# mLSTM cell and squared-ReLU FFN on one core: h computed with features in the rows, and FFN2 in two halves around FFN1

## Chip, core and metric

One core of a Trainium2 chip; the runs were spread over several chips, and each ratio below is against the kernel before on the same chip. The metric is the device time of the whole kernel in microseconds (us); lower is better. PE is TensorE (PEld its weight loads), DVE VectorE, ACT ScalarE, POOL GpSimd, SP SyncE, whose queue (SPq) issues the DMAs.

## The reference, cut

```python
# mLSTM cell, batch 4, heads 8, seq 768, head_dim 40; per step t:
C = f_stab * C + i_stab * outer(v, k);  n = f_stab * n + i_stab * k
y[:, :, t] = sigmoid(o) * (C q) / max(|n q|, 1)
# then, with x of 3072 tokens x 320:
h = maximum(x @ w_in, 0)        # 320 -> 2048
out = (h * h) @ w_out           # 2048 -> 320
```

## The kernel before: the parts that matter

Attention runs in 24 chunks `s` of 128 tokens (6 to a batch entry). FFN1 and FFN2 work on groups `g` of two chunks. All is float32. In attention, tokens stand in the rows of the result:

```python
def attend(s):                      # cut
    for j in range(PR):             # hi: state x q, 4 matmuls, 82 columns move
        nc.tensor.matmul(hi[:, 2*j:2*j+2, :]..., lhsT=d["qT"][:, j, :], rhs=C[:, j]...)
    for j in range(PR):             # dC: what the chunk adds to the state
        nc.tensor.matmul(dC[:, j]..., lhsT=d["kq"][:, 0, 2*j:2*j+2, :]..., rhs=d["vw"][:, 2*j:2*j+2, :]...)
    for h in range(H):              # hp: weights of 128 columns, 41 columns move
        nc.tensor.matmul(hp[:, h, :], lhsT=d["P"][h % 2][:, h // 2, :], rhs=d["va"][:, h, :])
    ...                             # DVE scales hi, masks dC; POOL adds to the state
```

FFN2 of groups 1 to 11 uses seven products in place of eight, from sums of blocks (`S1`, `S2`, `S4`, one more in place) that DVE makes. The products run in four steps, in two PSUM banks:

```python
elif step == 2:
    product(X5, S1, T[0]);                      add(u22, u22, X5)     # add: DVE reads PSUM
    product(Y6, g4[:, :, 1, cols[1]], T[2]);    add(m1, m1, Y6)
else:
    product(X5, S4, B22);                       add(u12, u12, X5)
```

The main loop deals out parts: four of FFN2(g), then four of FFN1(g+3), and so on. Each chunk of attention spans four parts: scores and P ahead of the first, attend and normalise ahead of the second, exponentials after the third. The sums are made in four short pieces inside FFN1. The order of an engine's instructions matters below: in these traces DVE and the DMA queue take theirs in the order of the program. A few names: `tp` holds the scores (k times q), P is the scores weighted by the decays, which DVE makes, and a *seam* is the stretch in which one group of FFN2 ends and the next begins.

## Time and profile before

| | before |
|---|---|
| time, median of 3 runs | 549.42 us (548.85 to 550.05) |
| span of the profiled run, mean granted clock | 546.6 us, 0.994 |
| PE busy | 537.6 us (98%) |
| DVE busy | 329.9 us (60%) |
| waits of PE for others after 98 us | one, of 0.9 us |

### The profile page before, as it was taken

What the parts mean: (1) busy time and instruction counts of PE and PEld (TensorE: products, weight loads), DVE (VectorE), ACT (ScalarE), POOL (GpSimd) and SP (SyncE); (2) the same over time, 40 slices, a digit from 0 to 9 for tenths busy, and PEclk for the clock granted to TensorE, in tenths of its full rate; (3) what the DMA queues carried; (4) which work ended last, traced back from release to release, by engine and by line L of the source; (5) the groups of instructions that cost most, each with busy time, mean ns of one, the idle gap of its engine ahead of it and who ended that gap; (6) DMA issues with size and microseconds to landing.
All of it is one profiled execution on the core that took longest, in us unless ns stands there. A gap on an engine that the chain in (4) does not pass through costs nothing.

```text
span 546.6 us, 9788 instructions
## 1 busy us (share of the span) xinstructions
PE 537.6 (98%) x3688; PEld 480.9 (88%) x3689; DVE 329.9 (60%) x637; ACT 176.6 (32%) x448; POOL 100.5 (18%) x117
## 2 busy tenths in 40 slices
PE   9989899999999999999999999999999999999997
PEld 5868788887889989989989989989989988979997
DVE  8588988788575575555565565555466456353440
ACT  3767587272242032341131432231423204011000
POOL 2354633233221120111121120101211210000000
PEclk9998999999999999999999999999999999999999
DMA  9998898856653654673565556466554220100000
GB/s 194 223 218 170 167 184 214 165 120 121 123 105 71 117 123 81 118 148 63 109 116 106 108 112 110 81 131 118 100 107 88 45 50 13 42 12 2 26 26 24
DMA packets 226480, 58.07 MB, mean 106 GB/s; under 512 B 185376, under 2 KB 223264, under 8 KB 226432
## 3 DMA queue, kind: packets, MB, share of 16 engines
q1 hardware_dynamic: 226336, 57.24, 52.8%
q8 instruction: 29, 0.48, 0.4%
q10 hardware_dynamic: 96, 0.20, 0.1%
q14 instruction: 19, 0.16, 0.1%
HBM read 49.84 MB, written 13.14 MB: 115 GB/s over the span
## 4 chain that ended last, share of the span: by engine, by line
PE 93%; DVE 4%; ACT 1%; issue 1%; POOL 0%; DVEq 0%; POOLq 0%
PE h_ps L619 31%; PE h_ps L525 29%; PE h_ps L536 8%; PE hp L446 8%; PE tp L409 4%; PE dC L439 3%; PE h_ps L565 3%; PE hi L432 3%; PE idle L682 1%; PE A_ps L348 1%; ACT W_sb L372 1%; DVE mag L203 1%; PE A_ps L344 1%; PE tp L396 1%; DVE g L558 1%
## 5 line engine op out<-in xcount | busy, mean ns | idle before, releaser
L525 PE MATMUL h_ps<-xT,w_in 128*128 128x256 f32 x768 | 175.5, 384 | 1.5 <-DVE xT L501 0.9
L525 PEld LDWEIGHTS h_ps<-xT,w_in 128*128 128x128 f32 x768 | 143.4, 190 | 24.7 <-issue 3.0
L551 ACT ACTIVATE r_sb<-h_ps 128x512 f32<-128x512 f32 x96 | 49.9, 601 | 196.7 <-PE h_ps L536 193.6
L558 DVE TENSOR_TENSOR g<-r_sb 128x512 f32<-128x512 f32 x96 | 62.4, 708 | 56.5 <-ACT r_sb L551 56.5
L619 PE MATMUL h_ps<-w_out,g 128*128 128x160 f32 x528 | 76.9, 302 | 0.0
L619 PEld LDWEIGHTS h_ps<-w_out,g 128*128 128x128 f32 x528 | 72.5, 190 | 1.3 <-ACT r_sb L551 0.3
L372 ACT ACTIVATE W_sb<-A_bc,b_T 128x128 f32<-128x128 f32 x176 | 53.8, 394 | 6.0 <-POOL A_bc L357 5.9
L619 PE MATMUL h_ps<-T,S 128*128 128x160 f32 x352 | 51.4, 299 | 0.0
L536 PE MATMUL h_ps<-xT,w_in 64*128 64x256 f32 x384 | 49.0, 391 | 0.0
L619 PEld LDWEIGHTS h_ps<-T,S 128*128 128x128 f32 x352 | 49.0, 190 | 0.0
L446 PE MATMUL hp<-va,P_sb 128*128 128x41 f32 x368 | 45.7, 286 | 0.0
L536 PEld LDWEIGHTS h_ps<-xT,w_in 64*128 64x128 f32 x384 | 34.8, 186 | 12.3 <-issue 9.0
L383 POOL TENSOR_TENSOR vw<-va,W_sb 128x328 f32<-128x328 f32 x20 | 16.3, 815 | 156.0 <-ACT W_sb L372 130.6
L446 PEld LDWEIGHTS hp<-va,P_sb 128*128 128x128 f32 x368 | 44.6, 198 | 0.0
L633 DVE TENSOR_TENSOR y_sb<-y_sb,h_ps 128x160 f32<-128x160 f32 x33 | 10.6, 320 | 48.9 <-PE h_ps L619 48.9
L465 POOL TENSOR_TENSOR C_sb<-C_sb,Cd 128x328 f32<-128x328 f32 x16 | 14.1, 878 | 124.1 <-DVE C_sb L457 123.8
L633 DVE TENSOR_TENSOR y_sb<-h_ps,y_sb 128x160 f32<-128x160 f32 x22 | 7.1, 324 | 45.1 <-PE h_ps L619 26.4
L421 DVE TENSOR_TENSOR P_sb<-tp,W_sb 128x512 f32<-128x512 f32 x46 | 29.5, 682 | 7.3 <-PE tp L409 6.8
L409 PEld LDWEIGHTS tp<-qT,kT 40*128 40x128 f32 x384 | 24.2, 187 | 3.3 <-issue 2.3
L409 PE MATMUL tp<-qT,kT 40*128 40x128 f32 x384 | 26.9, 279 | 0.0
L642 ACT COPY y_sb<-h_ps 128x160 f32<-128x160 f32 x11 | 3.2, 292 | 70.6 <-PE h_ps L619 70.6
L619 PE MATMUL h_ps<-T,g 128*128 128x160 f32 x176 | 25.7, 299 | 0.0
(100 smaller groups left out, 629.0 us busy)
## 6 DMA issues: line engine op xcount, KB each, us to landing
A_bc<-a_rows SPq DMA_DIRECT2D x22, 512.0 KB, 4.5
raw<-in_moe_w_out_dram SPq DMA_DIRECT2D x16, 320.0 KB, 3.3
raw<-in_moe_w_in_dram SPq DMA_DIRECT2D x8, 512.0 KB, 5.1
kq<-in_k_dram SPq DMA_DIRECT2D x24, 160.0 KB, 3.5
va<-in_v_dram SPq DMA_DIRECT2D x24, 160.0 KB, 4.0
og<-in_o_gate_dram SPq DMA_DIRECT2D x24, 160.0 KB, 3.8
out_dram<-y_sb SPq DMA_DIRECT2D x24, 160.0 KB, 2.5
x_rows<-x_sb SPq DMA_DIRECT2D x18, 192.0 KB, 2.1
```

The lines of the kernel that those rows point to most:

```text
L372: nc.scalar.activation(d["W"][:, i * n + h, :], A[i][:, h, :], AF.Exp, bias=b_T[:, b, c, i * n + h : i * n + h + 1],)
L409: nc.tensor.matmul(sc[i][:, j, :], lhsT=d["kT"][rows, j, :], rhs=d["qT"][rows, j, :], start=True, stop=True,)
L421: nc.vector.tensor_tensor(t, d["sc"][i], d["W"][:].rearrange("p (j two) t -> p j two t", two=2)[:, :, i, :], op=ALU.mult,)
L432: nc.tensor.matmul(hi[:, 2 * j : 2 * j + 2, :].rearrange("p h d -> p (h d)"), lhsT=d["qT"][:, j, :], rhs=C[:, j].rearrange("p h d -> p (h ...
L439: nc.tensor.matmul(dC[:, j].rearrange("p h d -> p (h d)"), lhsT=d["kq"][:, 0, 2 * j : 2 * j + 2, :].rearrange("p h d -> p (h d)"), rhs=d[" ...
L446: nc.tensor.matmul(hp[:, h, :], lhsT=d["P"][h % 2][:, h // 2, :], rhs=d["va"][:, h, :], start=True, stop=True,)
L525: nc.tensor.matmul(hs[i][:, n, :], lhsT=w_in[:, a, fb * P : (fb + 1) * P], rhs=xT[:, :, a, :], start=(n == 0 and a == 0), stop=False,)
L536: nc.tensor.matmul(hs[i][:, n, :], lhsT=w_in2[rows, 2 * pp + n, :], rhs=xT[rows, :, 2, :], start=False, stop=(n == 1),)
L551: nc.scalar.activation(rs[-1][:], h[:], AF.Relu)
L558: nc.vector.tensor_tensor(g4[:, :, i, :], r[:], r[:], op=ALU.mult)
L619: nc.tensor.matmul(to, lhsT=lhsT[:, p], rhs=rhs[:, p, :], start=(start and p == 0), stop=(p == NPAIR - 1), skip_group_check=True,)
L633: add = lambda to, a, b: nc.vector.tensor_tensor(to, a, b, op=ALU.add)
```

## The change

The intent: hp costs 109 ns a pass because 128 columns of weights are loaded to move 41. If v and the state become the weights (64 columns) and P and q move (128 columns), two heads fit beside each other in the array. The result then has features in the rows, so it is turned: DVE transposes 32x32 blocks, a store and four loads through DRAM move the blocks. That takes time, so x comes later, and FFN1 is put between the halves of FFN2. The diff, cut to its core:

```diff
+def attend_turned(s):
+    for j in range(PR):
+        for i in range(2):          # 64x64 tiles (0,0) and (64,64)
+            nc.tensor.matmul(numT[halves[i], j, :], lhsT=C[live[i], j*D1 : j*D1+DP], rhs=d["eA"][live[i], j, :], ...)
+    for j in range(PR):
+        for i in range(2):          # 128x64 tiles side by side
+            nc.tensor.matmul(numT[halves[i], j, :], lhsT=va_w[s % NKQ][:, h*D1 : h*D1+DP], rhs=d["P"][i][:, j, :], ...)
+    ...                             # dC likewise, 40 columns of weights, 41 move
+    nc.vector.transpose(tn..., numT...)
+def scale_q(s):                     # ahead of attend: eA (exponentials, by ACT) times q
+    nc.vector.tensor_tensor(d["eA"], d["eA"], d["qT"], op=ALU.mult)
+def move_num(s):                    # store tn to DRAM, four loads back
+def normalise_turned(s):            # two parts after attend
 ...
 elif step == 2:
-    product(X5, S1, T[0]);  add(u22, u22, X5)
-    product(Y6, g4[:, :, 1, cols[1]], T[2]);  add(m1, m1, Y6)
+    product(Y, g4[:, :, 1, cols[1]], T[2], start=True);  add(m1, u22, Y)
+    product(X, S1, T[0], start=True);  add(u22, u22, X)
 else:
-    product(X5, S4, B22);  add(u12, u12, X5)
+    product(X, S4, B22);  add(u12, u12, X)
 ...
-for g in range(NG):
-    parts += [(2, g, i) for i in range(4)] + FFN1(g + 3)
+for g in range(1, NG):
+    parts += [(2, g, 0), (2, g, 1)] + FFN1(g + 2) + [(2, g, 2), (2, g, 3)]
 ...                                 # and, at step 3 of each group:
+if new_sums:
+    for one in (1, 2, 3):
+        sums(g + 1, slice(0, NPAIR), (one,))
+if at == 3:
+    do(normalise_turned, s); do(store_rows, s)
```

More of the change, by code (lines that the diff above doesn't have):

```diff
@@ L92 @@
     kq_d = nc.dram_tensor("kq_rows", (NT, 2, 2, PR, P, D), F32, kind="Internal").ap()
+    n_d = nc.dram_tensor("num_rows", (NT, P, 4 * P), F32, kind="Internal").ap()
     x_d = nc.dram_tensor("x_rows", (NT, 3, P, P), F32, kind="Internal").ap()
@@ L97 @@
     kq_b = [consts.tile([P, 2, H, DP], F32, name=f"kq{i}") for i in range(NKQ)]
-    va_b = [consts.tile([P, H, D1], F32, name=f"va{i}") for i in range(NKQ)]
-    NKT = 3
-    kT_b = [consts.tile([P, PR, P], F32, name=f"kT{i}") for i in range(NKT)]
+    va_w = [consts.tile([P, H * D1 + 24], F32, name=f"va{i}") for i in range(NKQ)]
+    va_b = [t[:, : H * D1].rearrange("p (h d) -> p h d", d=D1) for t in va_w]
+    NKT = 2
+    kqT_b = [consts.tile([P, 2, PR, P], F32, name=f"kqT{i}") for i in range(NKT)]
     ident = consts.tile([P, P], F32)
-    bdm = consts.tile([P, PR, 2, D1], F32)
+    bdm = conv.tile([P, PR, 2, D1], F32, bufs=1)
     keep = gates.tile([BH, NB, P], F32)
@@ L115, in make_consts @@
             nc.vector.memset(t[:, :, D:], 1.0)
+        for t in va_w:
+            nc.gpsimd.memset(t[:, H * D1 :], 0.0)
         nc.vector.memset(keep[:], 1.0)
@@ L279, in pair_up @@
                 nc.sync.dma_start(
-                    kq_d[s, n, i].rearrange("j (m r) d -> m j (r d)", r=8),
-                    src[b, i::2, c * P : (c + 1) * P, :].rearrange("j (m r) d -> m j (r d)", r=8),
-                )
-    def squares_in(s, n, dst):
-        for i in range(2):
-            for e in range(0, D, SQ):
-                w = min(SQ, D - e)
-                nc.sync.dma_start(
-                    dst[DP * i + e : DP * i + e + SQ].rearrange("p (b a) -> p b a", a=SQ)[:, :, :w],
-                    kq_d[s, n, i, :, :, e : e + w].rearrange("j (m r) a -> r (j m) a", r=SQ),
-                )
-    def q_squares(s):
-        return kq_b[s % NKQ][:, 1].rearrange("p h d -> p (h d)")
+                    kq_d[s, i, n].rearrange("j (m r) d -> m j (r d)", r=8),
+                    src[b, PR * i : PR * (i + 1), c * P : (c + 1) * P, :].rearrange("j (m r) d -> m j (r d)", r=8),
+                )
     def load(s):
@@ L301, in load, with kqT @@
             nc.sync.dma_start(dst, src[b, :, c * P : (c + 1) * P, :].rearrange("h p d -> p h d"))
+    def kqT(s):
+        t = kqT_b[s % NKT]
+        st[s]["kT"], st[s]["qT"] = t[:, 0], t[:, 1]
+        return t
     def load_squares(s):
-        if s < KQ_SQ + NKQ:
-            nc.gpsimd.memset(q_squares(s), 0.0)
-        t = st[s]["kT"] = kT_b[s % NKT]
-        squares_in(s, 0, t[:].rearrange("p j t -> p (j t)"))
-        squares_in(s, 1, q_squares(s))
+        t = kqT(s)[:].rearrange("p n j (m a) -> p (n j m) a", a=SQ)
+        for i in range(2):
+            for e in range(0, D, SQ):
+                w = min(SQ, D - e)
+                nc.sync.dma_start(
+                    t[DP * i + e : DP * i + e + SQ, :, :w],
+                    kq_d[s, i, :, :, :, e : e + w].rearrange("n j (m r) a -> r (n j m) a", r=SQ),
+                )
     def turn_kq(s):
-        d = st[s]
-        nc.vector.transpose(d["kT"][:].rearrange("p j t -> p (j t)"), d["kT"][:].rearrange("p j t -> p (j t)"))
-        d["qT"] = work.tile([P, PR, P], F32, name="qT")
-        nc.vector.transpose(d["qT"][:].rearrange("p j t -> p (j t)"), q_squares(s))
+        t = kqT_b[s % NKT][:].rearrange("p n j t -> p (n j t)")
+        nc.vector.transpose(t, t)
     def load_o(s):
@@ L359, in mask, with decays @@
         )
+    def decays(s):
+        if s % NB > 0:
+            e = st[s]["eA"] = kq_b[2 + s % 2][:, 1].rearrange("p (j two) d -> p j (two d)", two=2)
+            for i in range(2):
+                rows = slice(DP * i, DP * (i + 1))
+                nc.scalar.activation(e[rows], st[s]["A"][0][rows, PR * i : PR * (i + 1), :], AF.Exp)
     def weigh(s, masked=False):
@@ L365, in weigh @@
         d["W"] = prep.tile([P, H, P], F32, name="W_sb")
-        d["dec"] = prep.tile([P, H], F32, name="dec")
+        if s < X_SQ:
+            d["dec"] = prep.tile([P, H], F32, name="dec")
+        elif not masked:
+            decays(s)
         if len(A) == 1 and not masked:
@@ L374, in weigh @@
                 )
-            nc.scalar.activation(d["dec"][:, hh], A[i][:, :, P - 1], AF.Exp)
+            if s < X_SQ:
+                nc.scalar.activation(d["dec"][:, hh], A[i][:, :, P - 1], AF.Exp)
         values(s)
@@ L392, in transposes @@
         d = st[s]
+        kqT(s)
         for i, n in enumerate(("kT", "qT")):
@@ L398, in transposes @@
                 )
-            d[n] = work.tile([P, PR, P], F32, name=n) if i else kT_b[s % NKT]
-            (nc.scalar.copy if i == 0 or s in (0, *range(2, 7)) else nc.vector.tensor_copy)(d[n][:], tp)
+            (nc.scalar.copy if i == 0 or s in (0, *range(2, 7)) else nc.vector.tensor_copy)(d[n], tp)
     def scores(s, o=(False, False)):
@@ L420, in weighted @@
             d["P"].append(t)
-            nc.vector.tensor_tensor(
-                t, d["sc"][i], d["W"][:].rearrange("p (j two) t -> p j two t", two=2)[:, :, i, :], op=ALU.mult,
-            )
+            heads = slice(i, H, 2) if s < KQ_SQ else slice(PR * i, PR * (i + 1))
+            nc.vector.tensor_tensor(t, d["sc"][i], d["W"][:, heads, :], op=ALU.mult)
     def attend(s):
@@ L450, in attend @@
         if c > 0:
-            num = d["num"] = work.tile([P, H, D1], F32, name="num", bufs=1)
+            num = d["num"] = old.tile([P, H, D1], F32, name="num", bufs=1)
             nc.vector.tensor_tensor(
@@ L455, in attend @@
         if c + 1 < NB:
-            Cn = work.tile([P, PR, 2, D1], F32, name="C_sb")
+            Cn = old.tile([P, PR, 2, D1], F32, name="C_sb")
             nc.vector.tensor_tensor(Cn[:], dC[:], bdm[:], op=ALU.mult)
             if c > 0:
-                Cd = work.tile([P, H, D1], F32, name="Cd", bufs=1)
+                Cd = old.tile([P, H, D1], F32, name="Cd", bufs=1)
                 nc.gpsimd.tensor_tensor(
@@ L466, in attend, with decay_C @@
             st["C"] = Cn
+    def scale_q(s):
+        if s % NB > 0:
+            d = st[s]
+            nc.vector.tensor_tensor(d["eA"], d["eA"], d["qT"], op=ALU.mult)
+    def decay_C(s):
+        if s % NB > 0:
+            Cd = st[s]["Cd"] = attn.tile([P, PR, D1], F32, name="Cd", bufs=1)
+            nc.gpsimd.tensor_tensor(
+                Cd[:], C_b[(s - 1) % 2][:, : PR * D1].rearrange("p (j d) -> p j d", d=D1),
+                st[s]["eA"][:, :, P - 1 : P].to_broadcast([P, PR, D1]), op=ALU.mult,
+            )
@@ new lines, in attend_turned @@
+    def attend_turned(s):
+        b, c = divmod(s, NB)
+        d = st[s]
+        halves = [slice(DP * i, DP * (i + 1)) for i in range(2)]
+        live = [slice(DP * i, DP * i + D) for i in range(2)]
+        numT = ps_at.tile([P, PR, P], F32, name="numT", tag="at")
+        if c > 0:
+            C = C_b[(s - 1) % 2]
+            for j in range(PR):
+                for i in range(2):
+                    nc.tensor.matmul(
+                        numT[halves[i], j, :], lhsT=C[live[i], j * D1 : j * D1 + DP], rhs=d["eA"][live[i], j, :],
+                        start=(j == 0), stop=False, skip_group_check=True,
+                    )
+        for j in range(PR):
+            for i in range(2):
+                h = PR * i + j
+                nc.tensor.matmul(
+                    numT[halves[i], j, :], lhsT=va_w[s % NKQ][:, h * D1 : h * D1 + DP],
+                    rhs=d["P"][h % 2][:, h // 2, :] if s < KQ_SQ else d["P"][i][:, j, :],
+                    start=(c == 0 and j == 0), stop=True, skip_group_check=True,
+                )
+        if c + 1 < NB:
+            dC = ps_at.tile([P, PR, D1], F32, name="dC", tag="at")
+            for j in range(PR):
+                for i in range(2):
+                    h = PR * i + j
+                    nc.tensor.matmul(
+                        dC[live[i], j, :], lhsT=d["kq"][:, 0, h, :D], rhs=d["vw"][:, h, :], start=True, stop=True,
+                    )
+        tn = attn.tile([P, P // SQ, PR, SQ], F32, name="tn", bufs=1)
+        nc.vector.transpose(tn[:].rearrange("p m j r -> p j m r"), numT[:].rearrange("p j t -> p (j t)"))
+        d["tn"] = tn
+        if c + 1 < NB:
+            Cn = C_b[s % 2][:, : PR * D1].rearrange("p (j d) -> p j d", d=D1)
+            for rows in live:
+                if c > 0:
+                    nc.vector.tensor_tensor(Cn[rows], dC[rows], d["Cd"][rows], op=ALU.add)
+                else:
+                    nc.vector.tensor_copy(Cn[rows], dC[rows])
@@ new lines, in move_num @@
+    def move_num(s):
+        N = st[s]["N"] = kq_b[s % 2][:, 1].rearrange("p h d -> p (h d)")
+        nc.sync.dma_start(n_d[s], st[s]["tn"][:].rearrange("p m j r -> p (m j r)"))
+        for m in range(P // SQ):
+            nc.sync.dma_start(
+                N[m * SQ : (m + 1) * SQ].rearrange("p (e c) -> p e c", c=P),
+                n_d[s, :, m * P : (m + 1) * P].rearrange("(e p) c -> p e c", p=SQ),
+            )
+    def normalise_turned(s):
+        d = st[s]
+        N = d["N"].rearrange("p (g e j r) -> p g e j r", g=2, e=2, r=SQ)
+        R = D - SQ
+        den = N[:, :, 1, :, R]
+        dm = work.tile([P, H], F32, name="dm")
+        dm2 = dm[:].rearrange("p (g j) -> p g j", g=2)
+        nc.vector.tensor_scalar(dm2, den, scalar1=-1.0, scalar2=1.0, op0=ALU.mult, op1=ALU.max)
+        nc.vector.tensor_tensor(dm2, dm2, den, op=ALU.max)
+        nc.vector.reciprocal(dm[:], dm[:])
+        x = d["x"] = work.tile([P, 3 * P], F32, name="x_sb")
+        x3 = x[:, :DM].rearrange("p (h d) -> p h d", d=D)
+        x4, og = x[:, :DM].rearrange("p (g j d) -> p g j d", g=2, d=D), d["og"].rearrange("p (g j) d -> p g j d", g=2)
+        nc.vector.tensor_tensor(x4[:, :, :, :SQ], N[:, :, 0], og[:, :, :, :SQ], op=ALU.mult)
+        nc.vector.tensor_tensor(x4[:, :, :, SQ:], N[:, :, 1, :, :R], og[:, :, :, SQ:], op=ALU.mult)
+        nc.vector.tensor_tensor(x3, x3, dm[:].unsqueeze(2).to_broadcast([P, H, D]), op=ALU.mult)
+        nc.vector.tensor_copy(x[:, DM:], x[:, DM - KR : DM])
@@ L569, in ffn2 @@
         if part == 1:
-            y = ffn.tile([P, DM], F32, name="y_sb")
+            y = ffn.tile([P, DM], F32, name="y_sb", bufs=3)
             nc.scalar.copy(y[:], o_ps)
@@ L626, in ffn2_fast @@
         if step == 0:
-            st["o2"] = [ps_h.tile([P, W], F32, name="h_ps") for _ in range(2)], [ffn.tile([P, DM], F32, name="y_sb") for _ in range(2)]
-        (X, Y), (y0, y1) = st["o2"]
+            st["y"] = [ffn.tile([P, DM], F32, name="y_sb", bufs=3) for _ in range(2)]
+        if step in (0, 2):
+            st["o2"] = [ps_h.tile([P, W], F32, name="h_ps") for _ in range(2)]
+        (X, Y), (y1, y0) = st["o2"], st["y"]
         g4 = st["g2", g][:].rearrange("p (f two) t -> p f two t", two=2)
@@ L631, in ffn2_fast @@
         S1, S2, S4 = st["S"]
-        X1, X5, Y6 = X[:, :DH], X[:, DH : 2 * DH], Y[:, :DH]
+        X, Y = X[:, :DH], Y[:, :DH]
         add = lambda to, a, b: nc.vector.tensor_tensor(to, a, b, op=ALU.add)
@@ L635, in ffn2_fast @@
         if step == 0:
-            product(X1, g4[:, :, 0, cols[0]], B11, start=True)
-            nc.scalar.copy(m1, X1)
-            product(Y6, S2, T[1], start=True)
-            add(u12, Y6, m1)
+            product(X, g4[:, :, 0, cols[0]], B11, start=True)
+            nc.scalar.copy(m1, X)
+            product(Y, S2, T[1], start=True)
+            add(u12, Y, m1)
         elif step == 1:
-            product(X1, g4[:, :, 1, cols[0]], B21)
-            nc.scalar.copy(y0[:, :DH], X1)
-            product(Y6, g4[:, :, 0, cols[1]], B12)
-            add(u22, Y6, m1)
+            product(X, g4[:, :, 1, cols[0]], B21)
+            nc.scalar.copy(y0[:, :DH], X)
+            product(Y, g4[:, :, 0, cols[1]], B12)
+            add(u22, Y, m1)
         elif step == 2:
-            product(X5, S1, T[0])
-            add(u22, u22, X5)
-            product(Y6, g4[:, :, 1, cols[1]], T[2])
-            add(m1, m1, Y6)
+            product(Y, g4[:, :, 1, cols[1]], T[2], start=True)
+            add(m1, u22, Y)
+            product(X, S1, T[0], start=True)
+            add(u22, u22, X)
             t = g * GT + 1
@@ L652, in ffn2_fast @@
         else:
-            product(X5, S4, B22)
-            add(u12, u12, X5)
+            product(X, S4, B22)
+            add(u12, u12, X)
             t = g * GT
@@ L663, in weigh_on @@
     def weigh_on(s):
-        do(lambda s: weigh(s, masked=(s == 7)), s)
+        do(lambda s: weigh(s, masked=(s == KQ_SQ)), s)
         do(load_A, s + 2)
@@ L669, in score @@
         weighted(s)
-    def attend_on(s):
-        do(attend, s)
-        do(normalise, s)
+        scale_q(s)
     zeros = consts.tile([P, 16], BF16)
@@ L726 @@
     ffn = ctx.enter_context(tc.tile_pool(name="ffn", bufs=2))
+    before = ExitStack()
+    old = before.enter_context(tc.tile_pool(name="old", bufs=2))
     weighted(0)
@@ L817 @@
     ps_h = ctx.enter_context(tc.tile_pool(name="ps_h", bufs=5, space=PSUM))
-    parts = [(1, 2, i) for i in range(4)]
-    for g in range(NG):
-        parts += [(2, g, i) for i in range(4)]
-        if g + 3 < NG:
-            parts += [(1, g + 3, i) for i in range(4)]
+    before.close()
+    attn = ctx.enter_context(tc.tile_pool(name="attn", bufs=1))
+    C_b = [attn.tile([P, PR * D1 + 24], F32, name=f"C{i}") for i in range(2)]
+    for t in C_b:
+        nc.gpsimd.memset(t[:], 0.0)
+    parts = [(1, 2, i) for i in range(4)] + [(2, 0, i) for i in range(4)]
+    for g in range(1, NG):
+        parts += [(2, g, i) for i in range(2)]
+        if g + 2 < NG:
+            parts += [(1, g + 2, i) for i in range(4)]
+        parts += [(2, g, i) for i in range(2, 4)]
     for n, (which, g, i) in enumerate(parts):
@@ L825 @@
         if n == 1:
+            decays(s + 1)
             mask(s + 1)
@@ L832 @@
         if at == 1:
-            attend_on(s)
-            if s % GT == 1:
+            do(attend_turned, s)
+            if s > X_SQ:
                 do(turn_squares, s - 1)
@@ L837 @@
             sums_of_weights(n - 5)
+        if n == 6:
+            sums(1, slice(0, NPAIR), (1, 2))
+        if n == 8:
+            sums_of_weights(3)
+            sums(1, slice(0, NPAIR), (3,))
         if n == 9:
-            sums_of_weights(3)
-        if which == 1 and g > 2 and i in (0, 2):
-            sums(g - 2, slice(2 * i, 2 * i + 4))
-        if which == 2 and g >= NG - 3 and g + 1 < NG and i == 3:
+            sums(1, slice(0, NPAIR), (4,))
+        new_sums = which == 2 and 0 < g < NG - 1 and i == 3
+        if new_sums:
             for one in (1, 2, 3):
@@ L845 @@
         if at == 3:
+            do(normalise_turned, s)
+            do(store_rows, s)
             if s % 4 == 3:
@@ L865 @@
             ffn2_fast(g, i)
-        if which == 2 and g >= NG - 3 and g + 1 < NG and i == 3:
+        if new_sums:
             sums(g + 1, slice(0, NPAIR), (4,))
@@ L871 @@
             do(turn_kq, s + 1)
-        if at == 3 and s % GT == 1:
-            do(turn_squares, s)
+        if at == 3:
+            do(decay_C, s + 1)
         if n < 4:
@@ L877 @@
         if at == 1:
-            do(store_rows, s)
+            do(move_num, s)
             do(load, s + 4)
```

## The prediction

> **What bounds the kernel now.** I read, in this order: busy time by engine, the chain that ended last, that chain piece by piece, and the timelines of TensorE (PE) and VectorE (DVE) around one pair of chunks and in the last stretch. Busy time and the chain's shares:
>
> ```profile
> PE 537.6 (98%) x3688; PEld 480.9 (88%) x3689; DVE 329.9 (60%) x637; ACT 176.6 (32%) x448; POOL 100.5 (18%) x117
> ...
> PE 93%; DVE 4%; ACT 1%; issue 1%; POOL 0%; DVEq 0%; POOLq 0%
> ```
>
> PE is 98% busy and 93% of the chain. A busy PE may hide gaps, so I went to the chain in order of time (start, duration, engine, tile, line, number of passes). One period of two chunks begins:
>
> ```profile
> 184.74 1.09 PE tp L409 x16
> 185.83 3.65 PE h_ps L525 x16
> 189.48 0.85 PE hi L432 x8
> 190.33 0.89 PE dC L439 x8
> 191.23 1.75 PE hp L446 x16
> 192.98 3.53 PE h_ps L525 x16
> 196.51 1.93 PE h_ps L536 x16
> 198.44 7.10 PE h_ps L525 x32
> 205.54 1.93 PE h_ps L536 x16
> 207.47 0.89 PE tp L409 x16
> 208.36 4.54 PE h_ps L619 x32
> ```
>
> Each piece starts where the one before ended: from 98 to 478 us PE waits for nobody, and the time is the sum of the paces. A program matmul is two passes here (hp has 8 in the code, 16 in the trace). Paces per pass: hp 1.75/16 = 109 ns with 41 columns moving, hi and dC 106 to 111 ns with 82, FFN1 (L525) 222 ns with 256, FFN2's products (L619) 136 ns with 160, scores (L409) 0.89/16 = 56 ns with 128. FFN1 and FFN2 go with the columns that move, about 1.2 per ns. hi, dC and hp do not: 41 and 82 columns cost alike, so the loading of 128 columns of weights bounds them. Scores use 64-row halves of the array in pairs, and two of them run at once. The same list shows what a change of layout costs: tp takes 1.09 after a full-array matmul and 0.89 after L536, which is already in halves (0.2 us to go in); the L525 after tp takes 3.65 against 3.53 (0.12 us to come out), and L619 x32 after tp 4.54 against 32 x 136 = 4.37 (0.17).
>
> The second thing to read is what DVE does at the seam between two FFN2 groups. The timeline of PE, then that of DVE, in the last stretch (start, duration, operation):
>
> ```profile
> 508.44 2.34 PE L619 MATMUL h_ps<-T,g 128*128 128x160 f32 x16
> 510.62 2.34 PE L619 MATMUL h_ps<-w_out,S 128*128 128x160 f32 x16
> ```
>
> ```profile
> 508.70 0.32 DVE L633 TENSOR_TENSOR y_sb<-y_sb,h_ps 128x160 f32<-128x160 f32 x1 [1.91 <-PE h_ps L619]
> 510.82 0.32 DVE L633 TENSOR_TENSOR y_sb<-y_sb,h_ps 128x160 f32<-128x160 f32 x1 [1.79 <-PE h_ps L619]
> 511.06 1.22 DVE L614 TENSOR_TENSOR S<-g 128x1024 f32<-128x1024 f32 x1
> 512.31 1.22 DVE L614 TENSOR_TENSOR S<-S,g 128x1024 f32<-128x1024 f32 x1
> 513.45 1.22 DVE L614 TENSOR_TENSOR g<-g 128x1024 f32<-128x1024 f32 x1
> ```
>
> The addition that takes a product out of PSUM starts 0.26 us after the next product has begun (508.44 to 508.70) and ends at 0.58. Today another product lies between a bank's reader and its next writer, so PE never sees this. One sum of 1,024 elements moves DVE on by 1.14 to 1.25 us.
>
> **What the Trainium skill says.** "TensorE: Matmul & The Clock Gate", LDWEIGHTS (loading the stationary operand), gives the load as columns/1.2 ns: 128 columns 107 ns, 64 columns 53 ns. The trace agrees for 128 (hp 109 ns); no run here has 64. The same page, Part 3, says that matmuls in different column groups run at once, three of them 2.38 times as fast; this trace shows only row groups, 56 ns a pass against about 110, and no column groups. "TensorEngine Tiling (Array Packing)", Key Properties, says that changing the mode, not just the tile, drains the engine; the 0.2 and 0.12 to 0.17 us above agree. Its Gotcha 1: PSUM Pressure says different row tiles cannot access one PSUM bank at once; scores keep to two banks, but the new state product writes both its tiles to one bank, in different partitions. No run here shows what that does.
>
> **The change on PE.** It touches chunks 6 to 23: 18 chunks, 3 of them without a state before (no hi) and 3 without one after (no dC). Removed: 15 x 0.85 + 15 x 0.89 + 18 x 1.75 = 57.6 us. Added, if paired tiles run at once: the state part, 16 passes of 128 columns in 64x64 tiles, like scores: 0.89 plus 0.18 to go in, 15 x 1.07 = 16.1. The part with P, 16 passes in 128x64 tiles: 0.95 (a little less than perfect pairing) plus 0.18 for another mode, 18 x 1.13 = 20.3. The new dC, 16 passes of 41 columns with 40 of weights: estimated at 38 ns, 15 x 0.6 = 9. Coming out, 18 x 0.15 = 2.7. Sum 48.1, so PE is **9.5 us** better. FFN1 and FFN2 keep their numbers of passes, and the reordering keeps one score of each pair behind L536.
>
> **The change at the seams.** In the new FFN2 step 2 the product with S1 comes last, and step 3 adds S4's product onto the same bank. It must wait until DVE has read the bank. From the timeline above: 0.58 us plus a signal, about 0.65 us a group, groups 1 to 11: **+7.2 us**.
>
> Then DVE's queue, which is in order. I checked its order in the built kernel. Between step 2 of one group and the state product of the next even chunk it holds: the addition, the turn of k and q, three sums, the normalising of the odd chunk, an addition, the fourth sum, two P, and the new scaling of q. Today the sums lie in four short pieces inside FFN1. With t = 0 where step 3 would have begun: addition done 0.58; turn of 1,024 (today two of 512, 0.70 and 0.67, so 1.25) 1.8; three sums 3.5 to 5.35; normalising, today 1.73 to 1.9 without its first addition, to 7.2; addition 7.45; fourth sum 8.65; two P (1.28) 9.9; scaling of 512 elements (0.65) 10.55. PE meanwhile: step 3 from 0.65 to 2.8, scores to 3.9, step 0 (4.54) to 8.45. It then needs the scaled q, which comes 2.1 to 2.2 us later. This occurs for s = 10, 14, 16, 20, 22; for 12 and 18, which have no state, PE waits for P alone, 1.5 us. 5 x 2.2 + 2 x 1.55 = **14.1 us**. For odd chunks the same count gives no wait, barely: squares and P end 3.66 us after FFN1's end today, the scaling makes it 4.3, and PE arrives at 4.5.
>
> The turn of h over DRAM (a store of 256 KB, four loads, a normalising two parts later) should be hidden: the same shape for x takes about 6 us (2.1 us for the store, 2.3 for a load, and the issues), and two parts take 8 us or more. At the last FFN1 a wait of 0.9 us becomes about 1.3. DMA is 0.5 to 0.6 busy there and gains large packets only.
>
> Sum: 549.4 - 9.5 + 7.2 + 14.1 + 0.4 = 561.6. The guess on dC is the softest and could be 3 us too dear; I say **560 us**.
>
> **Rivals.** (1) DVE's queue does not hurt, because PE, or the compiler's order, is other than I count; then the saving stands alone. If mode changes also cost little and dC runs at 25 ns, PE saves about 20 us, and the time is 530 to 540. For it: a rewrite this large, with FFN2 moved around FFN1 to give the turn time, looks tuned to a purpose. Against it: 10.5 us of DVE work with measured durations against 8.45 us of PE work. (2) Column groups do not pair for f32, or two row tiles in one bank take turns. Then P costs 1.75 again (+14 us), or the state part does (+13 us): 573 to 587. For it: no run here has column groups, and the page's warning on banks. Against it: row groups do pair perfectly in f32. (3) The turn over DRAM arrives late and DVE stands at the normalising, dragging squares and sums with it: 1 to 2 us more for each of 18 chunks, 570 to 580. Against it: 6 us of latency in at least 8 us.
>
> **Range and chances.** Rival 1 in part (half the seam cost) gives 545 to 550; rival 2 in part gives 573 to 577. The range is 543 to 577. Faster by over 2% needs under 538.4, that is almost the whole best case of rival 1: 0.08. Slower by over 2% starts at 560.4, right at my sum, and the rivals above it weigh more than those below: 0.50. Within 2%: 0.42.
>
> **What would show it.** In the profile after: passes of the P part at 55 to 65 ns (109 would be rival 2), the state part near 56, dC below 45; PE waiting for DVE at the state product of even chunks, about 2 us, five times, with P at s = 12 and 18; some 0.6 us before each step 3; PE's busy time down by about 10 us while its idle time grows by 20. The prediction is wrong if PE shows no waits for DVE from chunk 8 on, or if DVE itself waits for the turned h.

## The result, and the profile after

The changed kernel takes **565.6 us** (median of 4 runs, 560.57 to 567.23) against 549.13: ratio 1.0288, 95% interval 1.0219 to 1.0358. Ratios here are the mean time of one kernel's fast runs over that of the other's in the same rounds, so not quite the ratio of the medians quoted. The control run below (e8) gave 563.99 us and 1.0274.

The page of the kernel after, busy time and shares of the chain that ended last:

```profile
PE 534.4 (95%) x3928; PEld 464.6 (82%) x3929; DVE 333.9 (59%) x620; ACT 193.1 (34%) x460; POOL 95.5 (17%) x110
...
PE 83%; DVE 9%; DMA 3%; ACT 2%; issue 1%; SPq 1%; POOL 0%; DVEq 0%; POOLq 0%; ACTq 0%
```

PE is hardly less busy, and its share of the chain has fallen from 93% to 83%. What PE waited for (total us, times, longest), kernel after:

```profile
PE numT L505 <- DVE kq L483: 15.4, 6, 4.0
PE h_ps L715 <- DVE y_sb L731: 4.5, 11, 0.4
...
PE numT L512 <- DVE P_sb L435: 0.8, 4, 0.3
```

numT L505 is the state product, kq L483 the scaled q; h_ps L715 behind y_sb is step 3 behind DVE's read of the bank. The chain in order of time for chunks 9 and 10 (start, duration, engine, tile, line, passes):

```profile
173.60 1.02 PE numT L505 x16
174.62 1.02 PE numT L512 x16
175.64 0.31 PE dC L522 x16
175.95 3.65 PE h_ps L621 x16
...
186.49 2.44 PE h_ps L715 x16
188.93 1.09 PE tp L422 x16
190.02 4.56 PE h_ps L715 x32
...
194.77 1.28 DVE P_sb L435 x2
196.05 0.61 DVE kq L483
...
196.80 1.09 PE numT L505 x16
197.89 1.29 PE numT L512 x16
199.18 0.55 PE dC L522 x16
199.73 5.64 PE h_ps L715 x32
```

Chunk 9, undisturbed: the state part and the P part take 1.02 us each and dC 0.31, 2.35 us for what took 3.49. The paired tiles do run at once: 16 passes of 128 columns in 1.02 us is 64 ns a pass with the change of layout included. Chunk 10: PE ends step 0 at 194.58, and the state product starts at 196.80. And then PE is slow: the P part takes 1.29, and 32 passes of FFN2 that take 4.54 us elsewhere take 5.64.

DVE's timeline over the same seam, with two lines of POOL's, shows the queue:

```profile
186.11 0.32 DVE L731 TENSOR_TENSOR y_sb<-y_sb,h_ps 128x160 f32<-128x160 f32 x1 [1.85 <-PE h_ps L715]
186.35 1.24 DVE L315 STREAM_TRANSPOSE kqT<-kqT 128x1024 f32<-128x1024 f32 x1
187.51 1.18 DVE L710 TENSOR_TENSOR S<-g 128x1024 f32<-128x1024 f32 x1
187.62 1.68 POOL L396 TENSOR_TENSOR vw<-va,W_sb 128x328 f32<-128x328 f32 x1 [2.56 <-DVE kqT L315]
188.73 1.65 DVE L710 TENSOR_TENSOR S<-S,g 128x1024 f32<-128x1024 f32 x1
189.26 1.44 POOL L488 TENSOR_TENSOR Cd<-C,kq 128x164 f32<-128x164 f32 x1
190.30 1.48 DVE L710 TENSOR_TENSOR g<-g 128x1024 f32<-128x1024 f32 x1
...
193.63 1.22 DVE L710 TENSOR_TENSOR S<-g,S 128x1024 f32<-128x1024 f32 x1
194.77 1.28 DVE L435 TENSOR_TENSOR P_sb<-tp,W_sb 128x512 f32<-128x512 f32 x2
195.97 0.68 DVE L483 TENSOR_TENSOR kq<-kq,kqT 128x512 f32<-128x512 f32 x1
```

From 186.11 to 196.65 DVE does not stop once. Where POOL works beside it, both are slow: POOL's product takes 1.68 us against 0.74 elsewhere in this trace, and DVE's sums 1.65 and 1.48. The Trainium skill, "SBUF — State Buffer", SBUF: two separate sides, says that the two engines share one pair of ports under an exclusive lock when DVE has two SBUF inputs; the trace agrees in kind. It is so at all five seams with a state product (POOL's product takes 1.57 to 1.79 us there). At chunk 12 that product (0.74 us) ends before the sums begin, the same two sums take 1.22 us each, and DVE reaches the normalising 4.90 us after its addition and not 5.60: by this reading POOL costs DVE 0.7 us of each of the five waits. No run moves POOL's product to test it.

Granted clock (the fraction after the busy times; start:end and length come first) in three stretches of the kernel after, from the view of windows:

```profile
196.80:198.50 1.70, 1.70 (x28) 1.53 (x30) 0.09 (x1) 0.00 (x0) 0.00 (x0) 1.00 0.18 29
198.50:201.90 3.40, 3.40 (x32) 3.31 (x29) 1.83 (x4) 0.00 (x0) 0.00 (x0) 0.50 0.61 169
201.90:205.20 3.30, 3.30 (x25) 3.30 (x25) 0.00 (x0) 1.44 (x3) 0.45 (x1) 1.00 0.29 82
```

The clock falls to 0.50 shortly after the wait (1.7 us here), stays there for 3.4 us and comes back. From the start of the state product to FFN1 takes 8.57 us at chunk 10 and 6.96 at chunk 20, where the clock did not fall: 1.6 us. The same happens at chunks 14, 16 and 22, and at chunk 7 with 1.7 us: 8.1 us in all in this run.

The first wait is another one. Timeline of the kernel after around chunks 6 and 7:

```profile
105.69 0.72 DVE L527 STREAM_TRANSPOSE tn<-numT 128x512 f32<-128x512 f32 x1
109.02 6.66 SPq L186 DMA_DIRECT2D raw<-in_moe_w_out_dram  x3
115.72 0.42 SPq L539 DMA_DIRECT2D num_rows<-tn  x1
...
122.70 0.17 DVE L553 TENSOR_SCALAR dm<-kq 128x8 f32<-128x8 f32 x1 [1.29 <-DMA kq<-num_rows]
```

The turned h of chunk 6 is ready at 106.4, but the store is issued at 115.72: the one DMA queue, in order, holds weight loads that wait for buffers. DVE then waits 1.29 us for the data at the normalising, with FFN1's squares, the rounding of weights and chunk 7's P queued behind it. PE stands 4.0 us. DVE also waits for the turned h of chunks 8, 12, 18 and 20, by 1.0 to 1.6 us (6.4 us in all five), but no wait of PE follows there.

The account, from these traces, in us:

| | predicted | measured |
|---|---|---|
| attention on PE | -9.5 | -17.0 (12 full chunks 1.02 each, 3 without state before 1.17, 3 without state after 0.44) |
| bank wait before step 3 | +7.2 | +7.4 (11 x 0.41 idle, and 2.44 against 2.18 for the product) |
| state product behind DVE, chunks 10, 14, 16, 20, 22 | +11.0 | +11.4 (15.4 less 4.0) |
| P behind DVE, chunks 12 and 18 | +3.1 | +0.8 |
| chunk 7: the turned h of chunk 6, and DVE's other work behind it | 0 | +4.0 |
| slow clock after waits | 0 | +8.1 |
| start (PE reaches the first FFN1 scores at 69.9 against 68.4) | 0 | +1.5, in this run |
| last FFN1 (its wait is 0.9 us before, 0.3 after) | +0.4 | -0.6 |

The right column sums to +15.6; the spans differ by 17.3, so 1.7 us are not accounted for.

### The profile page after: what moved, and what is told of

Same layout as the page of the kernel before. It is cut to its first block, busy times and chain, and to the rows that moved or that the text cites. A ratio compares the mean times of both kernels' runs of the same rounds, so it can differ in the third digit from the quotient of the medians.

```text
span 563.9 us, 10278 instructions
## 1 busy us (share of the span) xinstructions
PE 534.4 (95%) x3928; PEld 464.6 (82%) x3929; DVE 333.9 (59%) x620; ACT 193.1 (34%) x460; POOL 95.5 (17%) x110
## 4 chain that ended last, share of the span: by engine, by line
PE 83%; DVE 9%; DMA 3%; ACT 2%; issue 1%; SPq 1%; POOL 0%; DVEq 0%; POOLq 0%; ACTq 0%
PE h_ps L715 30%; PE h_ps L621 27%; PE h_ps L632 7%; PE numT L512 4%; PE tp L422 4%; PE numT L505 3%; PE h_ps L661 2%; DVE P_sb L435 2%; DVE g L654 2%; PE hp L458 1%; PE dC L522 1%; DMA num_rows<-tn 1%; DVE mag L210 1%; ACT W_sb L384 1%; PE tp L410 1%
## 5 line engine op out<-in xcount | busy, mean ns | idle before, releaser
L654 DVE TENSOR_TENSOR g<-r_sb 128x512 f32<-128x512 f32 x96 | 61.7, 701 | 76.4 <-ACT r_sb L647 76.4
L715 PE MATMUL h_ps<-w_out,g 128*128 128x160 f32 x528 | 78.4, 306 | 0.0
L715 PEld LDWEIGHTS h_ps<-w_out,g 128*128 128x128 f32 x528 | 73.9, 193 | 1.4
L358 POOL TENSOR_SCALAR_AFFINE_SELECT A_bc<-A_bc 128x1024 f32<-128x1024 f32 x22 | 25.7, 1168 | 222.3 <-ACT kq L368 128.5
L715 PE MATMUL h_ps<-T,S 128*128 128x160 f32 x352 | 51.4, 299 | 0.0
L715 PEld LDWEIGHTS h_ps<-T,S 128*128 128x128 f32 x352 | 49.0, 190 | 0.0
L527 DVE STREAM_TRANSPOSE tn<-numT 128x512 f32<-128x512 f32 x18 | 12.9, 717 | 41.5 <-PE numT L512 41.5
L396 POOL TENSOR_TENSOR vw<-va,W_sb 128x328 f32<-128x328 f32 x20 | 20.1, 1006 | 86.5 <-ACT W_sb L384 69.7
L505 PE MATMUL numT<-kq,C 40*64 40x128 f32 x240 | 18.5, 299 | 15.4 <-DVE kq L483 15.4
L715 PE MATMUL h_ps<-w_out,S 128*128 128x160 f32 x176 | 26.8, 306 | 4.5 <-DVE y_sb L731 4.5
L505 PEld LDWEIGHTS numT<-kq,C 40*64 40x64 f32 x240 | 14.5, 144 | 19.8 <-issue 12.6
L435 DVE TENSOR_TENSOR P_sb<-tp,W_sb 128x512 f32<-128x512 f32 x46 | 29.5, 682 | 1.9 <-PE tp L422 1.9
L715 PEld LDWEIGHTS h_ps<-w_out,S 128*128 128x128 f32 x176 | 24.2, 190 | 7.2 <-DVE y_sb L731 7.2
L731 DVE TENSOR_TENSOR y_sb<-y_sb,h_ps 128x160 f32<-128x160 f32 x33 | 10.5, 319 | 27.6 <-PE h_ps L715 26.6
L422 PEld LDWEIGHTS tp<-kqT 40*128 40x128 f32 x384 | 24.2, 187 | 3.3 <-issue 1.3
```

Source lines behind the costliest of these rows:

```text
L358: nc.gpsimd.affine_select(A[:], A[:], compare_op=ALU.is_ge, fill=-1e30, base=0, pattern=[[0, H], [1, P]], channel_multiplier=-1,)
L396: nc.gpsimd.tensor_tensor(d["vw"][:], d["va"][:], d["W"][:, :, P - 1 : P].to_broadcast([P, H, D1]), op=ALU.mult,)
L422: nc.tensor.matmul(sc[i][:, j, :], lhsT=d["kT"][rows, j, :], rhs=d["qT"][rows, j, :], start=True, stop=True,)
L435: nc.vector.tensor_tensor(t, d["sc"][i], d["W"][:, heads, :], op=ALU.mult)
L505: nc.tensor.matmul(numT[halves[i], j, :], lhsT=C[live[i], j * D1 : j * D1 + DP], rhs=d["eA"][live[i], j, :], start=(j == 0), stop=False, s ...
L654: nc.vector.tensor_tensor(g4[:, :, i, :], r[:], r[:], op=ALU.mult)
```

## The experiments

Theory after the first reading: PE's attention did become cheaper, and the seams between FFN2 groups gave it back, because PE's time and DVE's queue run side by side there and the later one counts; each such wait also costs clock. Rivals: the turn over DRAM holds DVE up; the clock falls by itself; the reordering alone is to blame. All kernels gave correct results.

### e1_sums_later: two of the four sums behind P and the scaled q

```diff
-        if new_sums:
-            for one in (1, 2, 3): sums(g + 1, ..., (one,))
         if at == 3:
             do(normalise_turned, s); do(store_rows, s)
+        if new_sums:
+            for one in (1, 2): sums(g + 1, ..., (one,))
 ...
+        # next part, after score(s): sums 3 and 4
```

> Only DVE's order at the seam changes: the normalising and two of the four sums stay ahead of the next chunk's P and scaled q, the other two sums come after them. Theory (DVE's queue holds up PE at the state product, and the clock falls after each such wait): the waits of numT for the scaled q at even chunks from 10 on go from about 11.4 us in all to under 2, the slowed stretches of clock after them (4 of about 1.6 us) go too, only the one at chunk 7 stays; time 546 to 551 against 565.6. Rival A (DVE stands because the h turned over DRAM lands late): nothing changes by more than 2 us. Rival B (the clock falls by itself, not after the wait): 553 to 556, with the granted clock still near 0.976.

Measured: **549.7 us** (20 runs), ratio 1.0025 [1.0009, 1.0041]. What PE waited for:

```profile
PE h_ps L715 <- DVE y_sb L731: 4.5, 11, 0.4
PE numT L505 <- DVE kq L483: 4.5, 1, 4.5
PE h_ps L621 <- DVE xT L597: 3.3, 5, 1.2
```

Of the six waits at the state product only the one at chunk 7 is left. Nothing but DVE's order was changed, and most of the loss is gone. Rivals A and B fall for chunks 10 to 22. A new, small wait appears: FFN1 for the turned x.

### e2_idle_fill: PE kept busy during the wait

```diff
+            if s % 2 == 0 and s > 8 and s % NB and s < NT:
+                idle(10)            # bf16 matmuls on zeros, ahead of the state product
             do(attend_turned, s)
```

> Ten bf16 matmuls on zeros (2.2 us at full clock) go into PE's queue just ahead of the state product of chunks 10, 14, 16, 20 and 22, where PE waits 2.2 us for DVE; DVE is not touched. Theory (part of the loss is a clock that falls after the idle stretch): PE stays busy, the clock stays at 1.0 there, C, P and the products after them run at full pace: about 1.6 us less for each event avoided, 3 to 5 events, so 558 to 562 with a granted clock of 0.985 or more. Rival (the clock does not matter; the wait alone costs): 565 to 568.

Measured: **558.38 us**, ratio 1.0176 [1.0151, 1.0201], granted clock 0.990 to 0.994 in its four runs. The stretch behind chunk 10's state product in this kernel, from the view of windows (columns as above):

```profile
197.00:202.00 5.00, 5.00 (x54) 4.95 (x51) 1.83 (x4) 1.44 (x3) 0.43 (x1) 1.00 0.38 109
```

The clock is 1.00 there, and the 32 passes of FFN2 take 4.54 us again. DVE's queue is unchanged; 7.2 us came back, 5.6 against the control, from the clock alone (four falls of some 1.6 us were seen in the kernel after). So where the clock falls, an idle stretch of about 2.2 us costs PE some 1.6 us more afterwards. This settles that the wait leads to the slow clock, not the reverse.

### e3_copy_out: the bank wait removed alone

```diff
-            product(Y, ..., T[2], start=True);  add(m1, u22, Y)
-            product(X, S1, T[0], start=True);   add(u22, u22, X)
+            product(X, S1, T[0], start=True);   nc.scalar.copy(once[:], X)
+            product(Y, ..., T[2], start=True);  add(m1, u22, Y)
+            add(u22, u22, once[:])
```

> The S1 product comes first again in step 2, ACT copies it out, and DVE adds the copy; step 3 no longer waits for DVE's read of the bank. The wait before step 3 (11 x 0.41 us idle, 0.65 with the refilling) goes. If the seam costs simply add up (my prediction): 565.6 - 7.2 = 558.4. If DVE's chain is what ends last at the seams with a state product (my theory now): PE arrives 0.65 earlier and waits that much longer at 5 seams, gain only at the six others, less a DVE chain that starts 0.2 later: 561 to 564.5, with the waits at numT up to about 3 us each.

Measured: **572.27 us**, ratio 1.0419 [1.0391, 1.0447]: slower than the kernel after by 6.7 us. Both expectations missed. What PE waited for:

```profile
PE numT L505 <- DVE kq L483: 21.6, 6, 4.2
PE numT L512 <- DVE P_sb L435: 3.1, 4, 1.4
```

The bank wait is gone from the list (4.5 us idle, 7.4 with refilling), and the waits behind DVE are longer by 6.2 and 2.3. Both of DVE's additions now come after step 2's last product (at chunk 10 the turn of q and k starts 0.76 us after it, against 0.26 before), so DVE's queue starts later while PE arrives earlier. The granted clock is 0.967 to 0.970 against 0.976, some 5 us more lost to it. 8.5 - 7.4 + 5 = 6.1 of the 6.7. The direction of my theory held (no gain where DVE ends last); its size did not, for I had counted neither the second addition fully nor the clock. (In this run's trace the clock falls after all six waits, three times for twice as long.)

### e4_first_later: chunk 6 normalised behind chunk 7's P

```diff
         if at == 0:
             do(score, s)
+            if s == 7:
+                normalise_turned(6); store_rows(6)
```

> Only chunk 6: its normalising moves behind the squares and the P of chunk 7. Theory (DVE stands for the turned h of chunk 6, whose store was issued 9 us late because the DMA queue was held by weight loads, and squares, P and PE wait behind it): the wait of 4.0 us at chunk 7 and the slow clock after it (1.7 us) go: 559 to 561. Rival (PE would wait there for other DVE work of that stretch anyway, such as the rounding of w_out): 564 to 566.

Measured: **562.81 us** (559.15 to 564.16), ratio 1.0242 [1.0202, 1.0282], against 1.0274 to 1.0288: about 2 us better, half of what was expected, and not clear of the noise, since the intervals overlap. What the trace shows is clearer. What PE waited for:

```profile
PE numT L505 <- DVE kq L483: 13.0, 6, 2.2
...
PE h_ps L621 <- DVE xT L597: 3.2, 2, 2.7
```

The wait at chunk 7 went from 4.0 to 1.9 us, what is left being DVE's squares and rounding of weights. But x of chunk 6 is now stored later, its loads hold the queue until the turned h of chunk 7 is late too, and FFN1 waits 2.7 us. So about half of the wait at chunk 7 came from the place of the normalising, as in the theory, and half from DVE's other work, as in the rival; and the move was not free.

### e5_seams: e1 and e3 together

Its diff is those two, and the turn of q and k for even chunks moved ahead of step 2's additions.

> The reordered sums of e1 and the copied-out bank of e3 together, and the turn of q and k of the even chunks a little earlier in DVE's queue. Theory (at the seam PE's time and DVE's queue run side by side, and the later one counts): with DVE's queue shortened below PE's time, the bank wait is at last worth its 0.65 us a group, which e3 alone could not show: 549.7 (e1) less up to 7.2, 541 to 546; less than the full gain if FFN1 then waits for the turned x, as it did by up to 1.2 us in e1. Rival (the copy out itself does harm, which made e3 slower): not below e1, 549 to 554.

Measured: **548.52 us**, ratio 0.9987 [0.9971, 1.0004]; 17 of 20 runs fast. That is 1.2 us better than e1, less than the theory's range. The copy does no harm once DVE's queue is short, so the rival falls, but the full 7 us did not come. Its profiled run was one of the three slow ones, so its waits are not used; e7, read below, points to the reason.

### e6_order_alone: the reordering without the turned attention

The kernel before, with the parts, the four steps and the sums at the seam of the kernel after; attention as before.

```diff
-    parts: FFN2(g, 0..3), FFN1(g + 3, 0..3)
+    parts: FFN2(g, 0..1), FFN1(g + 2, 0..3), FFN2(g, 2..3)
-            sums inside FFN1, in halves
+            sums(g + 1, ..., 1, 2, 3) ahead of step 3, (4) behind it
```

> The kernel before with only the second part of the change: FFN2 in two halves around FFN1, its sums at the seam, its bank order; attention stays as before. Theory: PE's attention costs what it did, the bank wait comes in at 11 x 0.65 us, and DVE's queue at the seam (about 8.1 us without the normalising and the scaling of q) just fits into PE's 8.45, so there is no wait at the state product: 554 to 558, granted clock 0.99 or more. Rival (the reordering alone already makes the wait at the seam): 562 or more, with waits of PE for DVE in attention.

Measured: **555.5 us**, ratio 1.0127 [1.0089, 1.0165]. What PE waited for:

```profile
PE h_ps L619 <- DVE y_sb L635: 4.6, 11, 0.4
```

There is no wait for DVE in attention after chunk 1: without normalising and scaling at the seam, DVE's queue fits. The reordering costs about 7 us (the interval is 5 to 9), which its bank wait explains (7.4 us with refilling, as in the kernel after). The remaining 8 to 10 us of the change's loss (against e8 and against the kernel after) come from the turned attention meeting that seam, and from chunk 7.

### e7_best: e5, chunk 6 rearranged, loads of odd chunks behind the store of x

```diff
         if n == 4:
+            (rounding of the last weights, normalise_turned(6), both behind score(7))
+            if s == 7: store_rows(6)            # in part 5, behind move_num(7)
-        if at == 2: load_squares(s + 2)         # odd s: one part after the next, at at == 0
```

> e5_seams, and chunk 6 normalised behind the P of chunk 7, the rounding of the last weights behind that P too, and the loads of q and k for odd chunks moved behind the store of x in the DMA queue. Theory: PE keeps the whole gain of the paired tiles, 57.6 us of attention becoming about 41 (18 chunks of 2.35 us or less), and waits for little: 532 to 538, faster than both kernels. Rival (some further wait takes the place of those removed, most likely FFN1 for the turned x): 539 to 545.

Measured: **546.09 us**, ratio 0.9958 [0.9921, 0.9995]: the rival's case, 1 us beyond its range. The shares of its chain by engine, then what the SP queue, DVE and PE waited for:

```profile
PE 48%; DVE 16%; DMA 15%; SPq 15%; issue 4%; ACT 2%; POOL 0%; DVEq 0%; POOLq 0%
```

```profile
SPq L590 <- DMA x_rows<-x_sb: 62.6, 18, 4.8
...
SPq L541 <- DMA num_rows<-tn: 38.3, 18, 3.7
```

```profile
DVE xT L597 <- DMA xT<-x_rows: 61.7, 16, 7.2
...
PE h_ps L715 <- DVE S L710: 6.0, 7, 2.0
```

SPq and DMA together hold 30% of the chain. L590 and L541 are the loads of x and of the turned h. Each load waits in the queue for its own store to land, 3.5 and 2.1 us on the mean, and everything behind it waits too. DVE then waits for x, and PE for the sums that DVE makes later: not for the turned x, as the rival had guessed first (2.2 us). That this took the place of the waits removed is so far only read from the trace; e11 tests it.

### e8_after_again: the control

> The changed kernel once more, on the chip of the three beside it, as a control: 561 to 568, and where single runs differ, the granted clock differs with them, by about 0.003 for each 1.7 us.

Measured: 563.99 us (561.35 to 566.93), ratio 1.0274 [1.0231, 1.0317]. Its runs order with their clocks: 561.35 at 0.988, 563.84 and 564.15 at 0.982, 566.93 at 0.976, about 1.4 us for each 0.003. So the spread of this kernel goes with the time at the low clock. Whether the clock falls after a wait varies: the profiled run of this same program has the same six waits, and the clock falls after three of them (chunks 7, 20 and 22; at 22 for 6.8 us), against five in the kernel after. In e4's profiled run it falls after two of six (14 and 20), which is why that run, at 0.994, was its fastest.

### e9_queue, e10_act_issues, e11_between: the DMA queue relieved

```diff
 # e10 and e9: four copies a chunk issued by ACT
-                nc.sync.dma_start(kq_d[s, i, n]..., src...)
+                (nc.scalar if s > 9 else nc.sync).dma_start(kq_d[s, i, n]..., src...)
 # e11 and e9: independent issues between a store and the loads that wait for it
     nc.sync.dma_start(n_d[s], tn...)
+    between()                       # loads of k, v, o for later chunks
     for m in range(4): nc.sync.dma_start(N[...], n_d[s, ...])
 ...
     nc.sync.dma_start(x_d[s]..., x...)
+    between()                       # loads of the turned q and k of chunk s + 2
     for r in range(4): nc.sync.dma_start(xT[...], x_d[s, ...])
```

> e7_best with the DMA queue relieved: the four copies of q and k into rows are issued by ACT, and between the store of the turned h (or of x) and the loads that wait for it stand issues that need not wait. Theory (in e7 the one DMA queue, in order, with about 20 us of issuing and waiting in each 21 us chunk, became the bound: DVE waits 20 us for the turned h and 62 us for x, and PE 6.0 us for the sums and 2.2 for x behind it): these waits of PE fall under 2 us in all and the time to 534 to 540, over 1.5% faster than before. Rival (DVE or the latency of the transfers themselves bounds the seams now): 543 to 547, as e7.

> e7_best with one half of e9: ACT issues the four copies of q and k (2.5 us of issuing a chunk leave the one queue), the order of the rest as in e7. If the sum of issuing and waiting in the queue is the bound, this half gives about 2.5 us of slack a chunk and most of e9's 9.7 us: 537 to 541. If it is the waiting of loads behind their own store, this half gives little: 543 to 546.

> e7_best with the other half of e9: the copies stay in the one queue, and issues that need not wait stand between the store of the turned h or of x and the loads that wait for it. These loads waited 38 and 63 us in all in e7. If that waiting is what fills the queue, this half gives most of e9's gain: 537 to 541; if the issuing itself is, it gives little: 543 to 546.

Measured: e9 **536.42 us**, ratio 0.9795 [0.9766, 0.9825]; e10 540.16 us, 0.9856 [0.9821, 0.989]; e11 **535.62 us**, 0.9759 [0.9743, 0.9776]. e11 is the best version: faster than both kernels, and faster than the kernel before by over 2% (e9's interval reaches across 2%). What its SP queue waited for, and what its PE waited for after the start-up:

```profile
SPq L542 <- DMA num_rows<-tn: 12.1, 11, 2.6
...
SPq L592 <- DMA x_rows<-x_sb: 5.0, 3, 1.8
```

```profile
PE h_ps L623 <- DVE xT L599: 1.3, 1, 1.3
...
PE h_ps L717 <- DVE S L712: 0.7, 1, 0.7
PE numT L505 <- DVE kq L483: 0.7, 1, 0.7
```

The loads' wait for the store of h fell from 38.3 to 12.1 us, and that of x from 62.6 to 5.0. Filling the wait with other issues gives all of e9's gain (the issues moved also come at another time, which no run separates from the filling); moving issues to ACT gives 60% of it and nothing on top. My either-or for e10 (little, if waiting is the cause) was too sharp: taking 2.5 us of issues a chunk out of a full queue also leaves room for the waiting. In e10's trace the loads wait for their own stores nearly as long as in e7 (57.9 and 34.1 us), but DVE waits for the turned x 25.5 us in place of 61.7.

## Why the prediction was right or wrong, point by point

**PE's saving: right in kind, too small.** Tiles pair as assumed. The mis-sized term is dC: estimated at 38 ns a pass, 0.6 us a chunk; it took 0.31 to 0.33, some 20 ns a pass. The P part was put at 1.13 and took 1.02, that is 0.13 more than the 0.89 of 16 paired passes of scores, where the prediction had 0.06 for imperfect pairing and 0.18 for the change of layout. The saving was 17 us, not 9.5. The sign named for it, PE's busy time down by 10 us, did not come: it fell by 3.2, in part because slow passes count as busy. The other sign did: PE's idle time grew by 20.5 us (from 9.0 to 29.5).

**The bank wait: right.** 0.65 us a group, 7.2 in all, was the estimate; 7.4 is the trace, and e6 shows it nearly alone (0.0127 of 549 us is 7.0).

**DVE's queue at the seam: right, the size with some luck.** Waits of 2.1 to 2.2 us at five chunks were worked out; 11.4 us over these five were measured, and e1 took them away by moving two sums. At chunks 12 and 18, 1.55 us each were expected and 0.8 us over four waits measured. The trace of chunk 12 shows why: without POOL beside its sums DVE has both P ready 9.3 us after the point where step 3 would have begun, not 9.9, and PE, there at 8.5, waits 0.25 us for the first P and 0.16 for the second, working between. So the queue as the prediction summed it was about 0.6 us too long. At the state seams (10.57 us measured at chunk 10, 10.55 predicted) POOL's product, which it did not count, put this back.

**Odd chunks wait for nothing: right** from chunk 9 on. The odd chunk 7 is the exception, by way of the next point.

**"The turn of h over DRAM should be hidden": failed once for PE.** From chunk 8 on it held for PE in the changed kernel. At chunk 6 it did not: the estimate of 6 us took the transfers and left out that the one queue was held by weight loads, 9 us before the store was issued. PE lost 4.0 us there, of which e4 took away 2.1 by moving the normalising; the rest is other work of DVE. This is the third rival, in one place of the 18. The sign that the prediction named for being wrong, that DVE itself waits for the turned h, came at five chunks (6.4 us in all). Once the seams were mended (e5, e7) the same queue became the bound throughout.

**What was missing: the clock.** No step spoke of it. After five of the six waits of over 2 us the granted clock fell in the profiled run, 1.6 to 1.7 us each, 8 us in all; e2 shows it by filling the waits.

So the mechanism at the seams was right, and that the time came out within 4 us of the sum of 561.6 is partly luck: 7.5 us more were saved than thought and 2.3 less lost behind P, and 12 us were lost in two places not thought of.

## What to carry to other kernels

A saving on the engine that bounds a kernel is only worth what the in-order queues beside it allow: add up, at each seam, the work that another engine must do between two points of the bounding engine, and compare it with the time in between. When a wait is found, remove the ones that run side by side together; removing one of two parallel delays alone made it worse here (e3). Do not let a load that needs a store stand directly behind it in a DMA queue that others need; put issues that need not wait between them.

## What the Trainium skill lacked or had wrong

- "TensorE: Matmul & The Clock Gate", Part 1, puts the fall of the clock to half after at least one idle window of about 3.4 us, and the page's last table (Why this matters for your kernels) advises against gaps over some 3 us. The half agrees (0.50, for 3.4 us a fall). The length of the gap does not: waits of 2.2 to 2.5 us were followed by a fall at four chunks of five here, and at two of five in each of the profiled runs of e8 and e4, 1.6 us lost each time that was measured.
- The same page, Part 3, gives pairing of column groups for three tiles; for two f32 tiles of 128x64 these runs show 64 ns a pass with the change of layout included, against 109 ns before. No page has a pace for f32 tiles with 40 columns of weights and 41 moving: 20 ns a pass in pairs.
- "TensorEngine Tiling (Array Packing)", Gotcha 1, says that different row tiles cannot access one PSUM bank at once. Two 64x64 tiles that write different partitions of one bank ran at once here: 1.02 us for 16 passes of 128 columns, the same as the 128x64 pairs, and correct.
- The same page, Key Properties, lets a change of tiling mode drain the engine and gives no time for it. Here it is 0.2 us from full array to halves and, estimated as 1.02 less 0.89 us for 16 paired passes, about 0.13 us between 64x64 and 128x64.
- No page says what it costs the other issues of a DMA queue that a load stands right behind the store it waits for: 3.5 us a time for x and 2.1 us for h in e7, and 10.5 us of the kernel's time between e7 and e11.
